# A new order of the instruction queues in a fused attention and gated-mixer kernel

## The chip, the cores and the metric

The kernel runs on one core of a Trainium2 chip. The core has five engines, each with its own instruction queue that is worked off in order: TensorE (PE) for matmuls, ScalarE (ACT), VectorE (DVE) and GpSimd (POOL) for elementwise work, and SyncE (SP), which here only issues DMAs. They wait for each other on semaphores. The metric is the device time of one execution in microseconds; the median of several runs counts, less is better.

## The reference

The input x has 2048 tokens of width 448. A vector c gives six modulation vectors. The first half is windowed attention with 16 heads of 28 columns, where a token sees itself and the 255 tokens before it; the second is a gated MLP whose gate mixes tokens by a full 2048 x 2048 matrix.

```python
mod = silu(c) @ w_mod                       # sa, ca, ga, sb, cb, gb
h = layernorm(x) * (1 + ca) + sa
q, k, v = split_heads(h @ wqkv)
scores = where(0 <= i - j < 256, q @ k.T * 28 ** -0.5, -1e9)
x = x + ga * (merge_heads(softmax(scores) @ v) @ wo)
h = layernorm(x) * (1 + cb) + sb
z = gelu(h @ w_in)                          # 1792 columns, two halves
g = w_sp @ layernorm(z[:, 896:]) + b_sp[:, None]
x = x + gb * ((z[:, :896] * g) @ w_out)
```

## The kernel before

The tokens are cut into 16 tiles of 128 rows (t or j) and 4 blocks of 512 (tb). Weights and x come by DMA, in the front on the queues of SP and ScalarE. There is one pass over the data, in stages that overlap:

- Front. c is turned into a column by four tiny matmuls with a constant `one`, silu is taken on ScalarE, and matmuls with w_mod (`wmod`) give the modulation. `stats` (L591 to L597) takes mean and variance of a tile of x on VectorE and the inverse root on GpSimd; `norm` (L604 on VectorE, L608 and L610 on GpSimd) writes the normalised tile `xn`.
- Transpose and projections. Block 0 and 1 are transposed on TensorE, blocks 2 and 3 by DMA transposes of `xn` on SP's queue; scale and shift follow (L655, L674) into `hT`. `wq` is copied from its staging tile into a padded `WQK` (L583, L584). L689 and L729 give queries and keys, L742 the values; their results are evicted from PSUM by ScalarE or VectorE (L703, L704, L746, L747). Part of the queries is spread into `QBD` by four small DMAs per block.
- Attention, for j = 0 to 15 in two halves: scores (L818, L844, L853), exp on ScalarE (L805), a multiply with the 0/1 mask on VectorE (L860, L880), the product with the values (L887), division by the sum (L901, L903), a DMA transpose of the result (`o_sb` to `hT`), the output projection with `wo_g` (L912), the residual sum (L917), the second layer norm, a DMA transpose of `xn2` to `hT`, and scale and shift (L935, L937).
- Gated block: L997 gives the gate's half of z (ScalarE gelu L1004, statistics and normalisation on VectorE and GpSimd), L1018 the other half, transposed (gelu L1026).
- Spatial product: L1041 multiplies with `w_sp`, whose 32 pieces (`wspA`, `wspB`) are transposed by DMA on SP's queue. VectorE adds the bias `bsp_bc` (L1045), GpSimd multiplies with z (L1048), L1058 is the last product with `w_out_g`, and VectorE adds the residual (L1068) ahead of the store.

Nothing in the program chooses the order at run time or by a rule. Each step is entered into a list by `Sched.add`, with its possible engines and the steps that it depends on, and gets a number. The string `ORDER` then says the rest: one word per step, such as `113.v.0`, gives the number, the engine (p TensorE, a ScalarE, v VectorE, g GpSimd, s SP) and the buffer or PSUM bank that it takes. The words of one engine, from first to last, are that engine's queue. The semaphore waits are derived from dependences and buffer reuse. Some steps may run on one engine alone; others (evictions, scale and shift, normalisation, small copies) have two or three ways. 28 of the 37 optional warm-up matmul steps are left out of the string, in both versions alike.

```python
for word in ORDER.split():
    n, eng, *slots = word.split(".")
    op, e = self.ops[int(n)], ENGS["pavgs".index(eng)]
```

The numbers that matter here: 0 to 20 are loads (1 and 2 the first x tiles, 11, 14 and 15 x blocks 1, 2 and 3, 3 to 5 the first part of wmod, 6 to 8 wq, 12 and 13 the rest of wmod, 16 and 17 wo, 18 to 20 w_in); 22 is the memset of `one`, 25 that of a padding of the wq staging tile; 41 turns c, 42 and 43 are silu(c); 103 to 106 copy wq into WQK; 125, 126, 129 and 130 write hT of block 0; 131 to 134 are its first projection; 214 to 221 and 268 to 275 are statistics of blocks 2 and 3, 236 to 239 the scale and shift of block 2, 240 to 246 projections of it; 323 and 324 the first scores and exp; 756, 757, 764 and 765 the last masks; 805 to 820 and 821 to 836 the transposes of wspA and wspB, 804 the load of the bias.

Of the kernel before, what the change touches and what calls it, by code (L numbers as in the profile page):

```python
# [22 lines left out]
126.v 131.p.5 59.p.0 132.p 133.p 134.p 136.p.3 135.a 138.p.4 46.a 48.v 146.p.1 147.a 164.v 162.v 168.v 163.v 166.v 167.v 165.v 169.v 170.g 171.g 139.a  # L23
142.p.0 143.a 150.s 172.g 151.s 149.s 176.g 174.g 178.g 173.g.0 179.g.1 140.p.2 141.a 137.a 148.s 14.s 16.s 15.s 18.s 17.s 154.p.1 152.p.0 323.p.0
155.v 144.p.1 153.v 145.v 95.p.0 324.a.0 177.v.2 96.v 325.v 175.v.3 327.v 156.p.1 329.p.0 157.a 330.a.1 47.a 97.p.0 98.v 180.p.1 326.p.0 348.p.0 328.p
183.p.0 377.p.0 181.v 182.v 92.p.1 349.a.2 350.a 355.p.0 356.a.3 357.a 331.v 184.v 333.v 185.v 214.v 351.v 94.v 93.v 218.v 158.p.0 332.p 192.p.1 334.p
159.v 186.p.0 375.p.0 193.a 187.a 376.a.4.0 219.v 216.v 27.v 217.v 220.v 215.v 221.v 190.p.1 188.p.0 358.v 335.v 353.v 336.v.0 272.v 191.v 274.v 360.v
273.v 379.v 380.v 270.v 352.p.0 354.p 222.g 223.g 224.g 226.g 228.g 225.g.0 227.g.1 230.g 231.g.2 229.g.3 189.a 378.a 337.s 383.p.0 359.p 160.p.0
385.p.0 198.p.1 361.p 384.a.5.1 161.a 386.a 404.p.0 199.v 362.v 363.v.1 200.p.0 204.p.1 381.p.0 406.p.0 405.a.6.2 407.a 268.v 201.v 409.v 205.v 271.v
388.v 269.v 275.v 387.v 408.v 232.s 235.s 234.s 233.s 196.s 194.s 195.s 197.s 412.p.0 382.p 212.p.0 414.p.0 202.p.1 213.v 413.a.0.3 203.a 433.p.0  # L30
389.p 390.p 210.p.1 208.p.0 434.a.1.4 415.a 209.a 441.p.0 442.a.2.0 417.v 391.v 392.v.2 416.v 410.p.0 411.p 418.p 419.p 437.v 211.v 238.v 435.p.0
206.p.0 276.g 102.g 277.g 101.g 239.g 282.g 236.g 99.g 284.g 280.g 278.g 285.g.0 283.g.1 279.g.2 281.g.3 100.g 420.v 237.v 438.v 421.v.0 436.a 207.a
462.p.0 463.a.3.1 443.p.0 246.p.1 439.p.0 244.p.0 470.p.0 245.v 247.a 444.a 471.a.4.2 240.p.1 464.p.0 242.p.0 440.p 465.a 241.v 445.v 466.v 243.v
475.v 467.v 446.v 491.p.0 492.a.5.3 364.s 393.s 422.s 20.s 447.p 472.p.0 252.p.1 258.p.0 259.v 253.a 499.p.0 473.a 394.p.1 493.p.0 254.p.0 448.p
500.a.6.4 520.p.0 494.a 255.a 521.a.0.0 474.v 495.v 395.v 449.v 450.v.1 496.v 289.s 249.s 287.s 288.s 286.s 451.s 251.s 248.s 250.s 260.p.1 365.p.0
468.p.0 501.p.0 469.p 502.a 261.v 366.v 504.v 528.p.0 476.p 477.p 522.p.0 256.p.1 264.p.0 367.v 478.v 479.v.2 368.v 503.v 525.v 293.v 292.v 524.v
529.a.1.1 257.a 523.a 549.p.0 550.a.2.2 497.p.0 338.p.1 498.p 505.p 530.p.0 506.p 290.g 339.v 291.v 507.v 532.v 533.v 508.v.0 265.a 531.a 557.p.0
558.a.3.3 298.p.1 551.p.0 262.p.0 526.p.0 578.p.0 552.a 299.a 263.v 554.v 562.v 396.v 553.v 527.p 534.p 266.p.0 559.p.0 423.p.1 579.a.4.4 586.p.0
560.a 267.a 583.v 424.v 535.p 536.v 537.v.1 425.v 580.p.0 452.p.0 300.p.1 587.a.5.0 581.a 340.v 426.v 561.v 453.v 341.v 591.v 397.v 582.v 342.g 398.g
399.g 400.g 555.p.0 556.p 588.p.0 301.a 589.a 607.p.0 294.p.1 296.p.0 563.p 609.p.0 608.a.6.1 615.p.0 19.s 480.s 509.s 538.s 297.a 401.g.0 343.g 590.v  # L40
612.v 295.v 564.p 565.v 566.v.2 610.a 617.p.0 616.a.0.2 618.a 481.p.0 482.v 510.p.1 454.v 611.v 483.v 511.v 636.p.0 306.p.0 584.p.0 585.p 592.p 593.p
638.p.0 637.a.1.3 639.a 302.s 303.s 304.s 305.s 567.s 644.p.0 307.v 484.v 594.v 427.g 344.g 402.g 403.s 428.g 345.g.1 512.v 595.v.0 619.v 455.v
310.p.1 311.v 620.v 308.p.0 346.g 369.g 370.g 429.g 485.g 456.g 371.g 645.a.2.4 646.p.0 309.a 647.a 613.p.0 665.p.0 539.p.1 316.p.0 667.p.0 614.p
621.p 347.s 430.g.2 431.g 432.s 596.s 513.v 648.v 640.v 514.g 457.g 515.g 372.g.0 486.g 487.g 516.g 373.g 649.v 641.v 517.g.1 666.a.3.0 668.a 673.p.0
622.p 540.v 317.v 675.p.0 568.p.1 314.p.0 674.a.4.1 676.a 694.p.0 623.v 541.v 624.v.1 642.p.0 696.p.0 643.p 650.p 651.p 669.v 695.a.5.2 315.a 697.a
569.v 677.v 312.p.1 670.v 570.v 652.v 653.v.2 571.v 542.v 458.g 572.g 543.g 805.s 459.g.2 544.g 518.g 625.s 374.s 654.s 488.g.0 545.g 788.g 489.g
573.g 574.g 791.g 702.p.0 597.p.0 704.p.0 671.p.0 678.v 672.p 679.p 680.p 699.v 698.v 598.v 681.v 703.a.6.3 313.a 707.v 682.v.0 599.v 706.v 705.a
723.p.0 724.a.0.4 320.p.1 318.p.0 725.p.0 700.p.0 731.p.0 319.a 726.a 701.p 708.p 709.p 626.p.0 733.p.0 732.a.1.0 321.a 734.a 752.p.0 519.s 683.s
490.s 728.v 727.v 546.g.1 547.g 710.v 655.p.1 460.v 711.v.1 736.v 735.v 789.g 790.g 627.v 656.v 600.v 601.g 575.g.0 576.g 729.p.0 730.p 737.p 738.p
754.p.0 753.a.2.1 755.a 760.p.0 756.v 739.v 740.v.2 757.v 602.g 684.p.0 758.p.0 762.p.0 759.p 761.a.3.2 763.a 837.p.0 838.p.1 657.v 764.v 628.v 658.v  # L50
685.v 712.s 548.s 461.s 659.g 629.v 765.v 603.g 630.g 604.g.1 660.g 631.g 661.g 632.g 792.v 793.a 794.a 713.p.1 766.p 767.p 714.v 795.v 768.v 769.v.0
686.v 322.s 741.s 577.s 770.s 839.p 840.p 841.a 848.a 873.p.3 874.p.2 875.p 876.p 891.p.0 892.p.1 893.p 877.a 884.a 895.a 742.p.0 771.p.1 894.p 902.a
981.p.2 855.p.0 982.p.1 605.v 633.g.2 842.v 634.g 662.v.0 849.v 715.v 687.v 843.v 716.v 606.s 635.s 688.g 663.g 689.g 717.g 718.g 690.g 719.g 691.g.1
743.v 744.v 878.v 745.v 772.v 692.v 664.s 773.v 746.g 747.g 748.g 749.v.2 897.v 774.v 720.v.0 693.s 806.s 797.v 721.v 799.v 796.g 775.g 776.g 903.v
750.v 787.g 777.g 722.s 751.s 850.v 778.v.1 779.g 879.v 886.v 781.g 780.s 896.v 885.v 880.v 851.v 887.v 888.g 889.g 890.v 801.v 803.v 819.s 813.s
811.s 820.s 815.s 808.s 817.s 816.s 814.s 810.s 807.s 818.s 809.s 812.s 798.a 856.p.3 857.p 858.p 859.a 866.a 983.p 984.p 800.v 802.g 904.v 905.v
# [1084 lines left out]
```

## Time and profile before

| | us |
|---|---|
| median of 3 runs | 279.58 |
| the three runs | 279.44, 279.58, 283.84 |
| span of the profiled execution | 281.0 |
| TensorE busy in it | 269.3 |
| VectorE busy | 164.3 |
| ScalarE busy | 128.5 |
| GpSimd busy | 126.1 |

The profile is one execution, its times count from the first instruction of the span. A group of instructions is named by the line of the code that issues it, its engine, and the tiles that it writes and reads. The lines of `stats` and `norm` are helpers' lines, shared by several stages. A gap ahead of an instruction is put down to the work whose semaphore came last. The end of a matmul is modelled, so the time from one start to the next is a better measure of a matmul's cost than its duration.

### The profile page before, as it was taken

To read this page: it belongs to the slowest core of one execution; us is meant where nothing else is said; L and a number is where in the kernel's file an instruction comes from. 1 tells how busy PE (TensorE), PEld (TensorE's weight loads), DVE (VectorE), ACT (ScalarE), POOL (GpSimd) and SP (SyncE) were. 2 spreads that over 40 slices of the span, in tenths; PEclk is the share of its full clock that TensorE was granted. 3 is DMA by queue.
4 is the path that set the end of the run, shared out by engine and by line. 5 is a ranking of instruction groups with operands and counts; after the bars stand their busy time and mean duration, and the time that the engine had idled before them with its cause. 6 is when DMAs were issued, how large, how long until landed. Compare 5 with 4: busy or idle time off the path is not lost.

```text
span 281.0 us, 7380 instructions
## 1 busy us (share of the span) xinstructions
PE 269.3 (96%) x3198; PEld 142.3 (51%) x3222; DVE 164.3 (58%) x355; ACT 128.5 (46%) x151; POOL 126.1 (45%) x200
## 2 busy tenths in 40 slices
PE   6799999799999999999999999999999999999995
PEld 2445556456657777544444444444444444444452
DVE  6347999599899999968898600000243003124443
ACT  4548899789999999866666700000000000000000
POOL 8231177921027989947769503001477101436110
PEclk9789999999999999999999999999999999999999
DMA  6775735343315485693699989910000000000032
GB/s 199 188 261 157 267 58 98 84 55 72 72 23 75 63 96 80 162 103 79 125 181 186 168 181 201 163 36 0 0 2 0 0 0 2 16 16 16 19 98 98
DMA packets 65347, 26.01 MB, mean 93 GB/s; under 512 B 56418, under 2 KB 64227, under 8 KB 65315
## 3 DMA queue, kind: packets, MB, share of 16 engines
q1 hardware_dynamic: 64496, 24.39, 43.6%
q10 hardware_dynamic: 818, 1.15, 1.5%
q8 instruction: 25, 0.41, 0.6%
q14 instruction: 8, 0.06, 0.1%
HBM read 9.01 MB, written 1.84 MB: 39 GB/s over the span
## 4 chain that ended last, share of the span: by engine, by line
PE 80%; POOL 5%; DVE 4%; ACT 4%; issue 3%; DMA 3%; ACTq 0%; POOLq 0%
PE ps L1041 34%; PE ps L997 8%; PE ps L1058 8%; PE ps L1018 8%; PE ps L689 6%; PE ps L887 4%; ACT PW L805 3%; PE ps L912 3%; DMA wmod<-in_w_mod_dram 3%; PE ps L844 2%; PE ps L742 2%; PE ps L853 1%; POOL xn L610 1%; PE ps L729 1%; POOL wo_g L580 1%
## 5 line engine op out<-in xcount | busy, mean ns | idle before, releaser
L805 ACT ACTIVATE PW<-ps 128x2048 bf16<-128x2048 f32 (+1 forms) x56 | 67.8, 1240 | 4.3 <-PE ps L844 2.6
L1048 POOL TENSOR_TENSOR z1T<-tmpg,z1T 128x512 bf16<-128x512 bf16 x28 | 31.7, 1152 | 77.9 <-DVE tmpg L1045 77.9
L1045 DVE TENSOR_TENSOR tmpg<-ps,bsp_bc 128x512 bf16<-128x512 f32 x28 | 19.0, 689 | 79.2 <-PE ps L1041 70.3
L1041 PE MATMUL ps<-wspB,z 128*128 128x512 bf16 x219 | 49.2, 379 | 0.3
L1041 PE MATMUL ps<-wspA,z 128*128 128x512 bf16 x219 | 48.9, 379 | 0.4 <-issue 0.2
L860 DVE TENSOR_TENSOR PT<-PW,mask 128x1024 bf16<-128x1024 bf16 x56 | 39.2, 729 | 0.3 <-ACT PW L805 0.2
L1041 PEld LDWEIGHTS ps<-wspA,z 128*128 128x128 bf16 x224 | 21.8, 98 | 26.6 <-issue 0.4
L1041 PEld LDWEIGHTS ps<-wspB,z 128*128 128x128 bf16 x224 | 21.9, 98 | 26.3
L596 POOL TENSOR_SCALAR ve_all<-mv_all 128x1 f32<-128x1 f32 (+2 forms) x37 | 11.3, 312 | 46.7 <-DVE mv_all L594 45.9
L689 PE MATMUL ps<-hT,WQK 128*128 128x512 bf16 x98 | 25.5, 388 | 2.4 <-POOL hT L655 1.4
L597 POOL TENSOR_TENSOR rs_all<-ve_all,neghalf 128x1 f32<-128x1 f32 (+2 forms) x37 | 25.3, 694 | 1.1
L887 PE MATMUL ps<-Vaug,PT 128*128 128x32 bf16 x496 | 24.4, 177 | 0.5 <-DVE PT L860 0.5
L887 PEld LDWEIGHTS ps<-Vaug,PT 128*128 128x128 bf16 x496 | 21.8, 96 | 4.4 <-DVE o_sb L903 0.9
L997 PE MATMUL ps<-w_in,hT 64*128 64x448 bf16 x224 | 22.7, 349 | 0.2 <-ACT PW L805 0.2
L1018 PE MATMUL ps<-hT,w_in 64*128 64x512 bf16 x196 | 22.3, 376 | 0.0
L1058 PE MATMUL ps<-w_out_g,z1T 128*128 128x448 bf16 x112 | 21.8, 353 | 0.0
L887 PE MATMUL ps<-Vaug,PW 128*128 128x32 bf16 x224 | 20.2, 176 | 0.0
L591 DVE BATCH_NORM_STATS2 st_all<-x_sb 128x6 f32<-128x448 bf16 x32 | 19.2, 610 | 0.4 <-DMA x_sb<-in_A_x_dram 0.4
L610 POOL TENSOR_SCALAR xn<-x_sb,rs_all,ve_all 128x448 bf16<-128x448 bf16 x22 | 18.9, 863 | 0.3
L887 PEld LDWEIGHTS ps<-Vaug,PW 128*128 128x128 bf16 x224 | 17.6, 96 | 1.9
L591 DVE BATCH_NORM_STATS2 st_all<-z 128x6 f32<-128x448 bf16 x32 | 18.1, 602 | 0.2 <-ACT z L1004 0.2
L1004 ACT ACTIVATE z<-ps 128x896 bf16<-128x896 f32 x16 | 14.1, 915 | 8.3 <-PE ps L997 8.2
(100 smaller groups left out, 333.1 us busy)
## 6 DMA issues: line engine op xcount, KB each, us to landing
out_dram<-fin SPq DMA_DIRECT2D x16, 112.0 KB, 1.7
x_sb<-in_A_x_dram SPq DMA_DIRECT2D x3, 448.0 KB, 4.9
wmod<-in_w_mod_dram SPq DMA_DIRECT2D x1, 1344.0 KB, 8.6
w_in<-in_B_w_in_dram SPq DMA_DIRECT2D x1, 1344.0 KB, 8.9
QBD<-qT SPq DMA_DIRECT2D x16, 64.0 KB, 2.0
w_out_g<-in_B_w_out_dram SPq DMA_DIRECT2D x1, 784.0 KB, 5.3
bsp_bc<-in_B_b_sp_dram SPq DMA_DIRECT2D x1, 512.0 KB, 6.8
wmod<-in_w_mod_dram SPq DMA_DIRECT2D x2, 224.0 KB, 6.1
```

Source lines behind the costliest of these rows:

```text
L591: st = [dve(0.62 if True else 0, lambda e, t=t, ci=ci, s=s: e.bn_stats(st_all[:, slot, t, ci, :], s()), deps(t), prio) for ci, s in enumer ...
L597: rs = pool(0.53 + 0.15 * len(tiles), lambda e: e.tensor_tensor(rs_all[:, slot, a:b], ve_all[:, slot, a:b], neghalf[:, 0:b - a], ALU.pow), ...
L610: "pool": (0.9, lambda e: e.tensor_scalar(to[:, h.slot[0], 0:D], x_sb[:, t, :], z, ve, ALU.mult, ALU.add))}, [nm], prio, [h])
L689: mms = [lambda e, h=h, g=g, kc=kc, tb=tb: e.matmul(ps[:, h.slot[0], :], lhsT=WQK[:, kc, 4 * g:4 * g + 4, :].rearrange("p a b -> p (a b)") ...
L805: ex = act(xdur, lambda e, out_ap=out_ap, in_ap=in_ap: e.activation(out_ap(), in_ap(), ACT.Exp, scale=SCALE), [s], v - 8.0 + u, takes, tab ...
L860: return dve(0.70, lambda e: e.tensor_tensor(cols(hp.slot[0] * 2048 + 1024 * k, [[256, 4], [128, 2], [1, 128]]), cols(at_w() + 128 + 192 * ...
L887: fns.append(lambda e, hp=hp, hO=hO, hi=hi, bi=bi, kb=kb, hd=hd, nb=nb, a=at[hi][bi], p_of=p_of: e.matmul(ps[:, hO.slot[0], 32 * hd:32 * h ...
L997: return lambda e, kc, p0, start, stop: e.matmul(ps[:, hs[t % 2].slot[hf], 0:D], lhsT=hT[p0:p0 + 64, kc, t * 128:(t + 1) * 128], rhs=w_in[ ...
L1018: return lambda e, kc, p0, start, stop: e.matmul(ps[:, hs[b // 2].slot[b % 2], :], lhsT=w_in[p0:p0 + 64, kc, ft * 128:(ft + 1) * 128], rhs ...
L1041: m = pe(16 * MMS, [lambda e, h=h, si=si, ft=ft, tb=tb: e.matmul(ps[:, h.slot[0], :], lhsT=z2[:, si, ft * 128:(ft + 1) * 128], rhs=(wspA i ...
L1048: u = pool(1.16, lambda e, ht=ht, ft=ft, tb=tb: e.tensor_tensor(z1T[tb][:, ft, :], tmpg[:, ht.slot[0], :], z1T[tb][:, ft, :], ALU.mult), [ ...
L1058: return [lambda e, ft=ft: e.matmul(ps[:, h.slot[0], 0:D], lhsT=z1T[t // 4][:, ft, (t % 4) * 128:(t % 4 + 1) * 128], rhs=w_out_g[:, ft, :] ...
```

## The change

Only `ORDER` is replaced. The two strings hold the same 1145 steps, so the same matmuls, elementwise instructions and DMAs run, on the same data, with the waits derived again. Two things differ: the place of a step in its engine's queue, and for 58 steps the engine. 19 steps go from GpSimd to VectorE and 11 from VectorE to GpSimd; 15 go from ScalarE to VectorE and 13 from VectorE to ScalarE. No step is moved to or from TensorE and SP. The buffers and banks that steps take are chosen anew with the order.

The first lines of the two strings show the front, the next the place where the projection of block 2 begins, then the end of attention, and the last the transposes of w_sp:

```diff
-2.a 21.v 30.g 1.s 22.v 23.v 24.v 33.g 34.g 0.a 4.s 31.g 3.a 28.g 25.v 5.s 32.g 6.a 26.v 35.g 50.v 51.p.0 7.s 40.a 8.s 52.p.1 36.g 107.v 53.p.2 109.v
-37.g 108.v 115.v 41.p.0 29.g 38.g 110.v 54.p.3 117.v 39.g 42.a 111.g 43.a 116.v 112.g 118.v 44.a 55.p.4 119.g 113.v.0 45.a 56.p.5 120.g 114.v.1
-123.p.1 9.s 121.v.2 49.p.0 122.v.3 10.s 105.a 11.s 106.a 127.p.2 12.s 103.v 104.g 124.p 88.v 128.p 89.v 90.v 13.s 91.v 57.p.3 125.a 129.v 58.p.4 130.a
...
+0.a 24.v 1.s 2.a 15.s 3.a 17.s 30.g 31.g 4.s 32.g 35.g 58.p.0 5.s 7.s 59.p.0 107.v 34.g 14.s 55.p.0 115.v 29.g 8.s 52.p.0 33.g 28.g 21.v 109.v 37.g
+40.a 36.g 53.p.0 108.v 117.v 54.p.0 110.v 23.v 118.v 111.g 274.v 57.p.0 112.g 22.v 41.p.0 51.p.1 39.g 42.a 113.v.0 43.a 44.a 114.v.1 56.p.1 116.v
+270.v 119.g 123.p.1 120.g 268.v 6.a 127.p.2 45.a 38.g 9.s 122.v.2 49.p.0 121.v.3 11.s 272.v 10.s 25.v 220.v 105.a 12.s 218.v 13.s 103.a 104.v 124.p
+20.s 216.v 128.p 50.v 88.v 106.a 89.v 90.v 91.v 125.v 126.v 129.a 131.p.3 132.p 130.v 133.p 47.a 26.v 134.p 271.v 168.v 140.p.4 164.v 46.a 166.v
...
+407.a 197.s 281.v.3 417.v 208.p.1 442.a.2.0 289.s 237.v 389.p 388.v 414.p.0 244.p.0 416.v 337.s 415.a 209.v 390.p 245.a 462.p.0 391.v 408.v 240.p.1
...
+736.v 726.a 760.p.0 576.g 321.a 627.v 754.p.0 577.s 730.p 757.v 755.a 737.p 738.p 761.a.3.2 762.p.0 739.v 684.p.1 322.s 756.v 657.v 713.p.0 740.v.0
+792.a 837.p.0 765.v 741.s 763.a 658.v 838.p.1 764.v 794.a 659.g 714.v 603.g 793.a 758.p.0 660.g 685.v 759.p 795.g 766.p 767.p 839.p 661.g 768.v
...
+820.s 885.v 892.p.3 859.a 843.v 893.p 745.v 878.v 812.s 746.g 981.p.0 692.g 895.a 861.v 747.g 774.v 879.v 894.p 775.g 798.a 810.s 776.g 799.v 858.p
...
+1035.a 1022.p.1 853.g 833.s 972.g 854.v 1014.p.0 944.v 962.v 823.s 1023.p 865.v 973.v 1015.p 1026.a 908.v 825.s 1024.p 1025.a 1016.p 830.s 1043.p.4
+1020.a 1019.a 1027.a 836.s 1017.a 1018.a 1028.a 829.s 1079.p.5 827.s 834.s 828.s 1040.p.0 822.s 826.s 1088.p.1 804.s 824.s 821.s 1082.p.6 1080.v.0
```

More of the change, by code (lines that the diff above doesn't have):

```diff
@@ L24 @@
[L24 to L47, printed above, removed]
@@ new lines @@
+146.p.0 135.a 48.v 214.v 141.a 138.p.5 273.v 147.a 217.v 27.v 167.v 169.v 136.p.1 162.v 139.a 163.v 275.v 165.v 142.p.0 170.g 137.a 171.g 323.p.0
+143.v 156.p.1 324.a.0 178.g 221.v 176.g 150.s 144.p.0 177.g.0 157.v 148.s 219.v 172.g 215.v 269.v 152.p.1 174.g 145.v 151.s 175.g.1 149.s 154.p.0
+179.v.2 153.a 222.g 173.v.3 16.s 223.g 329.p.0 155.v 97.p.1 18.s 330.a.1 327.v 19.s 276.g 180.p.0 226.g 98.v 348.p.0 181.v 95.p.1 349.a.2 182.v
+377.p.0 96.v 183.p.0 350.a 92.p.1 99.g 184.v 185.a 230.g 224.g 355.p.0 93.v 331.v 190.p.0 356.a.3 277.g 325.v 94.v 353.v 192.p.1 231.v.0 191.a 284.g
@@ L73 @@
+1162.p 1124.p.1 1159.v.3 1163.v.1 1160.s 1129.s 1125.v.2 1164.s 1126.s
 """
```

64 lines of the change are left out of this document (38 added, 26 removed).

## The prediction

> **What bounds the kernel now.** The page's list of busy times comes first, because it says which engine a new order has to serve.
>
> ```profile
> PE 269.3 (96%) x3198; PEld 142.3 (51%) x3222; DVE 164.3 (58%) x355; ACT 128.5 (46%) x151; POOL 126.1 (45%) x200
> ```
>
> TensorE is busy in 269.3 of 281.0 us, so an order alone can win back at most some 11.7 us, if no matmul goes faster. But the share is an average. The table by stage (columns: stretch, length, then the busy time and count of PE, PEld, DVE, ACT and POOL, the granted clock, DMA share, GB/s) shows where the loss is and who sets the pace:
>
> ```profile
> 0.00:18.50 18.50, 13.99 (x82) 6.88 (x84) 10.55 (x35) 8.71 (x12) 7.93 (x21) 0.82 0.78 241
> 18.50:30.10 11.60, 11.30 (x134) 6.03 (x132) 7.06 (x17) 9.29 (x12) 3.63 (x8) 1.00 0.56 171
> 30.10:57.00 26.90, 24.84 (x528) 14.45 (x536) 23.46 (x53) 23.95 (x26) 18.99 (x26) 1.00 0.49 106
> 57.00:116.60 59.60, 58.24 (x1476) 39.38 (x1479) 57.89 (x118) 55.08 (x56) 32.52 (x53) 1.00 0.43 68
> 116.60:160.30 43.70, 43.54 (x439) 21.00 (x439) 37.13 (x92) 29.57 (x45) 31.29 (x66) 1.00 0.88 150
> ```
>
> ```profile
> 160.30:278.20 117.90, 117.33 (x550) 54.54 (x558) 27.66 (x44) 1.93 (x4) 31.72 (x28) 1.00 0.25 49
> ```
>
> From 116.6 us to 278.2 TensorE stands still for 0.16 + 0.57 us. That tail of 161.6 us is full, and an order can only lengthen it. Everything to be won lies before 116.6, in the attention stage, where VectorE is the fullest engine: 57.89 of 59.6 us in the long stretch, and ScalarE 55.08. "A busy PE" says little there, since its small matmuls are pipelined and their ends modelled. The end of that stage is one instruction, the last mask multiply, and TensorE goes on with the gated block's first product right behind the matmuls that wait for it:
>
> ```profile
> 115.94 0.66 DVE L860 TENSOR_TENSOR PT<-PW,mask 128x1024 bf16<-128x1024 bf16 x1
> ```
>
> ```profile
> 117.40 2.82 PE L997 MATMUL ps<-w_in,hT 64*128 64x448 bf16 x28
> ```
>
> So I forecast when VectorE finishes that mask. Its ledger up to 116.6 us is 10.55 + 7.06 + 23.46 + 57.89 = 98.96 us busy, and idle 7.95 + 4.54 + 3.44 + 1.71 = 17.64 us. The chain of waits (start, length, what) names the two idle pieces that an order can touch:
>
> ```profile
> 1.94 7.71 DMA wmod<-in_w_mod_dram
> ...
> 15.55 5.63 PE ps L689 x23
> ...
> 50.67 1.52 POOL hT L655
> 52.19 0.35 issue
> 52.54 0.81 PE ps L689 x3
> ```
>
> The front waits for a weight load and then for the first query/key projection (L689) at 15.55. At 52.5 the projection of token block 2 waits for its normalised input, which GpSimd scales (L655) after its statistics came late: both VectorE and TensorE lose time around there.
>
> **The front, where the change costs.** Only the queues' order differs, so each step is costed by what now stands ahead of it. On SP's queue the load of x block 3 (448 KB) and a 56 KB piece of wo now stand behind the first x piece and ahead of SP's two pieces of wmod; x block 2 (448 KB) goes ahead of the last piece of wq. On ScalarE's queue the 448 KB piece of wq, issued at 2.37 us, moves behind the two small activations that make silu(c). On VectorE, a `bn_stats` of x block 3 goes ahead of the memset of `one`, and others of blocks 3 and 2 ahead of the copy of wq into WQK. Those queues are in order, so silu(c), and with it the issue of that piece of wq, now wait for x block 3.
>
> ```profile
> x_sb<-in_A_x_dram SPq DMA_DIRECT2D x3, 448.0 KB, 4.9
> ...
> wq_st<-in_A_wqkv_dram ACTq DMA_DIRECT2D x1, 448.0 KB, 8.7
> ...
> wspA<-in_B_w_sp_dram SPq DMA_TRANSPOSE x16, 4.2
> ```
>
> ```profile
> 2.37 0.49 ACTq L409 DMA_DIRECT2D wq_st<-in_A_wqkv_dram  x1
> ...
> 23.61 1.02 ACT L805 ACTIVATE PT<-ps 128x1024 bf16<-128x1024 f32 x1
> ```
>
> ```profile
> 0.88 0.06 DVE L478 MEMSET one<- 1x2 bf16 x1
> ...
> 12.60 1.00 DVE L674 TENSOR_SCALAR hT<-ps,modT 128x512 bf16<-128x512 bf16 x2 [0.83 <-PE ps L660]
> ```
>
> Issued near 1.3 us, x block 3 lands after 4.9 us (the median of the three loads of its size) at 6.2, or after 8.7 (the same size in the crowded front) at 10.0. I take 8.5: the first x pieces and ScalarE's wmod share the engines with it. One statistic, the memset (now at 9.2 instead of 0.88), four tiny matmuls and two small activations later, the piece of wq is issued at some 10.3 us instead of 2.37; it lands at 15.2 to 19.0, where it landed at 2.37 + 8.7 = 11.1. I take 15.6, near the short end, because the competing wmod piece is done by then. Behind it VectorE still copies WQK, does a statistic and five small copies, and makes the four hT chunks that were made at 12.60: the first L689 comes at some 17.6 us, 2.1 later than 15.55, with 21 as the far end. Two units of four matmuls are moved behind the first scores, worth 8 x 5.63 / 23 = 2.0 us, but TensorE idles longer ahead of L689 and its clock drops again (0.82 over the first 18.5 us before, 3.3 us lost). So the first exp comes at about 25 (23.7 to 27), not 23.61.
>
> [...]
>
> **VectorE's ledger with the change.** Fifty-eight instructions change engine; VectorE gets 34 and gives 24. What does not cancel is five normalisations, one scale-shift of the second block, three evictions of queries or keys and two of values to VectorE, and one small copy away from it. In groups (busy, mean ns | idle before):
>
> ```profile
> L860 DVE TENSOR_TENSOR PT<-PW,mask 128x1024 bf16<-128x1024 bf16 x56 | 39.2, 729 | 0.3 <-ACT PW L805 0.2
> ...
> L747 DVE CAST Vaug<-ps 128x448 bf16<-128x448 f32 x7 | 4.3, 615 | 4.0 <-PE ps L742 4.0
> ...
> L604 DVE TENSOR_SCALAR xn<-x_sb,mv_all,rs_all 128x448 bf16<-128x448 bf16 x10 | 4.1, 431 | 3.5 <-DMA hT<-xn 2.1 <-POOL rs_all L597 0.8 <-POOL ve_all L608 0.6
> ...
> L937 DVE TENSOR_SCALAR hT<-hT,modT 128x512 bf16<-128x512 bf16 x7 | 4.1, 608 | 0.0
> L704 DVE CAST KT<-ps 128x512 bf16<-128x512 f32 x6 | 4.1, 680 | 0.7 <-PE ps L689 0.7
> ```
>
> 5 x 0.431 + 0.608 + 3 x 0.680 + 2 x 0.615 = 6.0 us; less the copy, and less the part in which one instruction starts before the last one ends, I take 5.0. All of it stands ahead of the last mask.
>
> Idle time: the first stretch keeps its 7.95 us nearly (7.0, the waits have other names); the second keeps 4.0 of 4.54, since the first exp is later though the statistics of blocks 2 and 3 are already done; the third falls from 3.44 to 1.0, because with those statistics done early the normalised block 2 is transposed sooner and the wait at 52.5 goes; the fourth keeps 1.71. Together 13.7 us. What is late next in the third stretch is VectorE itself: it scales three chunks of block 2 there only after it has worked off the masks queued ahead.
>
> [...]
>
> ```profile
> 43.35 0.66 DVE L860 TENSOR_TENSOR PT<-PW,mask 128x1024 bf16<-128x1024 bf16 x1
> ...
> 47.53 2.14 DVE L860 TENSOR_TENSOR PT<-PW,mask 128x1024 bf16<-128x1024 bf16 x2
> ```
>
> ```profile
> 47.67 1.45 POOL L580 TENSOR_TENSOR wo_g<-wo_g,gg_sb 128x448 bf16<-128x448 bf16 x1
> ```
>
> A mask takes 0.66 us alone; two took 2.14 while GpSimd's multiply ran. Over 56 masks the mean of 0.729 is 3.9 us above 0.66. An order that takes turns saves between 0 and those 3.9 us and GpSimd has eight instructions fewer; new pairs can also cost as much. I take 2.5 saved. [...]
>
> Last mask: 98.96 + 5.0 + 13.7 - 2.5 = 115.2 us, 1.4 earlier than 116.6.
>
> **Behind it, at nothing.** The 14 transposes of wspA that end the queue are cover that could fail:
>
> ```profile
> 135.54 19.94 SPq L467 DMA_TRANSPOSE wspA<-in_B_w_sp_dram  x14
> ```
>
> The last is issued by 155.48 and lands 4.2 us later, just ahead of the spatial product at 160.3; three of them now stand in SP's gaps ahead of the last hT transposes, so they end sooner by about 3 x 1.42 us. If a late hT blocked SP, each us beyond 0.6 would be paid in full. The bias load moves behind 13 transposes of wspB, 18.5 us; its first reader has eight banks of 16 matmuls of cover, 128 x 117.33 / 550 = 27.3 us, and so does wspB, now first used in the ninth unit rather than the tenth. The reordered final products cost nothing while they find their bank free a unit ahead. The tail stays 161.6 us.
>
> **The sum.** The profiled execution spans 281.0 us against a median of 279.58 of the runs, 1.4 more. 281.0 - 1.4 = 279.6 in the profile; less the same 1.4 it is **278.2 us**.
>
> **Rivals.** *The front decides (slower).* Place: ScalarE's piece of wq behind VectorE's wait for x block 3. If x lands at 10 and wq takes 8.7 us in a front where SP's queue is still full, the first L689 comes at 21 or later, and the second stretch's idle time grows by about 4 us that nothing makes up, since VectorE has 5 us more work: 98.96 + 5.0 + 17.7 - 2.5 = 119.2, time 282.2. It decides against me from a first L689 at about 19.5. For it: ScalarE's wq piece took 8.7 us before. Against it: idle time there was paid before too. [...] *SP's transposes become the bound*: a wait of 3 us ahead of the spatial product gives 281.2. [...]
>
> **Numbers.** Forecast 0.42, front 0.28, freed middle 0.16, SP 0.06, port unchanged 0.08. The forecast's own range, from its unknown terms (first L689 17 to 19, port 0 to 3.9), is 276 to 281. For 8 in 10 I take 274.5 to 283.0, from the freed middle to past the front's 282.2. About 2% is what a measurement of this kernel can tell from no change: under 274.0 needs more than the freed middle (0.07), over 285.2 needs the front's far end with a stall behind it (0.12); within 2%: 0.81.
>
> **What would show it.** In the changed profile: first L689 near 17.6 and first exp near 25 (over 19.5: the front rival); no wait for L655 near 52; masks with a mean near 0.69 us; the last mask near 115; TensorE full from there to the end. I am wrong if the last mask is early but gaps stand behind it, or if it is late though the front was not.

## The result and the profile after

| | before | after |
|---|---|---|
| median, 18 executions each, same chip | 279.93 us | 282.24 us |
| lowest to highest | 278.75 to 283.84 | 281.50 to 283.19 |
| ratio of the times, 95% interval | | 1.0079 (1.0056 to 1.0101) |
| span of the shown profile | 281.0 us | 279.8 us |
| time of that execution | not given | 281.53 us |

The kernel became 0.8% slower, 2.2 us (279.93 x 0.0079). The forecast was 278.2, a little faster. The time lies in the range of 274.5 to 283.0, and within 2% as was thought likeliest, but on the wrong side of no change.

The two profiles say the opposite: after's span is 1.2 us shorter. The table by stage of after, with the columns and stretches of before's (stretch, length, busy time and count of PE, PEld, DVE, ACT and POOL, granted clock, DMA share, GB/s):

```profile
0.00:18.50 18.50, 10.52 (x76) 5.18 (x78) 13.46 (x38) 9.41 (x13) 6.88 (x20) 0.91 0.93 304
18.50:30.10 11.60, 11.60 (x112) 5.56 (x109) 9.20 (x28) 8.35 (x10) 6.08 (x13) 1.00 0.40 117
30.10:57.00 26.90, 25.98 (x596) 16.36 (x603) 23.76 (x51) 23.98 (x24) 10.36 (x16) 1.00 0.45 94
57.00:116.60 59.60, 58.83 (x1474) 40.04 (x1479) 57.70 (x122) 56.73 (x58) 28.63 (x53) 1.00 0.47 80
116.60:160.30 43.70, 43.47 (x412) 20.33 (x408) 33.76 (x86) 28.57 (x45) 27.90 (x62) 1.00 0.85 147
160.30:278.20 117.90, 115.73 (x544) 53.81 (x550) 28.24 (x44) 1.30 (x3) 33.75 (x30) 1.00 0.20 44
```

And the end of its attention stage in the timeline (start, length), with the group of masks from the page:

```profile
112.73 0.68 DVE L860 TENSOR_TENSOR PT<-PW,mask 128x1024 bf16<-128x1024 bf16 x1
113.42 0.66 DVE L860 TENSOR_TENSOR PT<-PW,mask 128x1024 bf16<-128x1024 bf16 x1
...
115.49 2.82 PE L997 MATMUL ps<-w_in,hT 64*128 64x448 bf16 x28
```

```profile
L860 DVE TENSOR_TENSOR PT<-PW,mask 128x1024 bf16<-128x1024 bf16 x56 | 37.1, 688 | 0.0
```

Inside these profiles the change did nearly what was forecast: the masks' mean fell from 729 to 688 ns, GpSimd's busy time from 30 to 57 us from 18.99 to 10.36, and the last mask ends at 114.08 instead of 116.6 (forecast 115.2). The forecast span was 279.6, the measured one is 279.8. So what failed is mainly the way from the profile to the median, and the first experiment was put there.

The slices of TensorE's clock show where to look. Before, between 10.24 and 20.48 us (columns as above):

```profile
10.24:13.65 3.41, 3.41 (x36) 2.54 (x36) 1.65 (x7) 2.41 (x4) 1.15 (x1) 0.50 0.71 163
13.65:17.07 3.42, 3.20 (x9) 1.29 (x9) 1.51 (x4) 0.51 (x2) 0.00 (x0) 0.54 1.00 376
17.07:20.48 3.41, 3.41 (x18) 1.57 (x16) 1.41 (x6) 2.32 (x5) 1.69 (x4) 1.00 0.55 190
```

After, the same slices:

```profile
10.24:13.65 3.41, 1.66 (x37) 1.35 (x34) 3.12 (x7) 1.79 (x3) 0.73 (x2) 1.00 1.06 360
13.65:17.07 3.42, 0.86 (x3) 0.38 (x5) 3.18 (x13) 3.42 (x5) 0.00 (x0) 0.71 1.04 391
17.07:20.48 3.41, 3.41 (x14) 1.46 (x13) 3.27 (x12) 2.41 (x4) 0.00 (x0) 0.79 0.61 163
```

Both executions ran part of the front at half clock (0.50 in before's first slice; 0.71 and 0.79 are slices that are partly at half: the clock of after is 0.50 from 16 to 18 us and 1.00 from 19). In after TensorE is nearly idle from 12.1 to about 16 us and slow after that. Whether that is a property of each kernel or of the execution that was profiled, one profile can't say.

### The profile page after: what moved, and what is told of

The parts are those of the page before. It is cut to its first block, busy times and chain, and to the rows that moved or that the text cites. A ratio compares the mean times of both kernels' runs of the same rounds, so it can differ in the third digit from the quotient of the medians.

```text
span 279.8 us, 7377 instructions
## 1 busy us (share of the span) xinstructions
PE 266.1 (95%) x3196; PEld 141.3 (50%) x3222; DVE 166.1 (59%) x365; ACT 128.3 (46%) x149; POOL 113.6 (41%) x192
## 4 chain that ended last, share of the span: by engine, by line
PE 81%; DVE 9%; DMA 4%; ACT 2%; issue 1%; POOL 1%; ACTq 0%; DVEq 0%; POOLq 0%
PE ps L1041 34%; PE ps L689 8%; PE ps L1058 8%; PE ps L887 5%; PE ps L1018 5%; PE ps L997 4%; PE ps L844 4%; PE ps L912 4%; PE ps L742 4%; DVE st_all L591 3%; DMA hT<-xn 2%; PE ps L853 2%; ACT PW L805 2%; DMA x_sb<-in_A_x_dram 2%; PE ps L729 1%
## 5 line engine op out<-in xcount | busy, mean ns | idle before, releaser
L860 DVE TENSOR_TENSOR PT<-PW,mask 128x1024 bf16<-128x1024 bf16 x56 | 37.1, 688 | 0.0
L1041 PEld LDWEIGHTS ps<-wspB,z 128*128 128x128 bf16 x224 | 21.9, 98 | 26.4
L689 PE MATMUL ps<-hT,WQK 128*128 128x512 bf16 x96 | 24.8, 393 | 5.5 <-DVE hT L674 4.1
L597 POOL TENSOR_TENSOR rs_all<-ve_all,neghalf 128x1 f32<-128x1 f32 (+2 forms) x37 | 25.9, 704 | 1.4
L596 POOL TENSOR_SCALAR ve_all<-mv_all 128x1 f32<-128x1 f32 (+2 forms) x37 | 10.2, 278 | 37.3 <-DVE mv_all L594 34.2
L887 PE MATMUL ps<-Vaug,PT 128*128 128x32 bf16 x496 | 23.8, 177 | 0.0
L887 PEld LDWEIGHTS ps<-Vaug,PT 128*128 128x128 bf16 x496 | 21.8, 96 | 3.9 <-DVE o_sb L903 0.6
L887 PE MATMUL ps<-Vaug,PW 128*128 128x32 bf16 x224 | 19.8, 176 | 0.0
L887 PEld LDWEIGHTS ps<-Vaug,PW 128*128 128x128 bf16 x224 | 17.5, 96 | 2.1
L689 PEld LDWEIGHTS ps<-hT,WQK 128*128 128x128 bf16 x112 | 10.2, 100 | 15.7 <-DVE hT L674 4.5
L1026 ACT ACTIVATE z1T<-ps 128x512 bf16<-128x512 f32 x28 | 14.8, 602 | 5.8 <-PE ps L1018 5.7
```

The costliest lines, as they stand in the source:

```text
L597: rs = pool(0.53 + 0.15 * len(tiles), lambda e: e.tensor_tensor(rs_all[:, slot, a:b], ve_all[:, slot, a:b], neghalf[:, 0:b - a], ALU.pow), ...
L689: mms = [lambda e, h=h, g=g, kc=kc, tb=tb: e.matmul(ps[:, h.slot[0], :], lhsT=WQK[:, kc, 4 * g:4 * g + 4, :].rearrange("p a b -> p (a b)") ...
L860: return dve(0.70, lambda e: e.tensor_tensor(cols(hp.slot[0] * 2048 + 1024 * k, [[256, 4], [128, 2], [1, 128]]), cols(at_w() + 128 + 192 * ...
L887: fns.append(lambda e, hp=hp, hO=hO, hi=hi, bi=bi, kb=kb, hd=hd, nb=nb, a=at[hi][bi], p_of=p_of: e.matmul(ps[:, hO.slot[0], 32 * hd:32 * h ...
L1041: m = pe(16 * MMS, [lambda e, h=h, si=si, ft=ft, tb=tb: e.matmul(ps[:, h.slot[0], :], lhsT=z2[:, si, ft * 128:(ft + 1) * 128], rhs=(wspA i ...
```

## The experiments

### Is the profile of before like its median?

Before, unchanged.

> The kernel before, unchanged, for the span of each of its executions. After's profile spans 279.8 us at a time of 281.53, so 1.73 us lie outside its span. Theory A (the profile of before was one of its slow executions): with the same 1.73 outside, before's median of 279.93 means spans of about 278.2, and the shown 281.0 is reached only by the executions near 282 to 283. Theory B (the two kernels differ outside the span): spans here stay near 281.0 with a time near 280, that is under 1 us or nothing outside.

Measured: 280.67 us, ratio 1.0002 (0.9982 to 1.0023), and for every execution about 1.7 to 1.8 us between span and time. That is theory A. Over all 108 executions of before that ran beside the experiments, by mean granted clock:

| clock | executions | median time, us | time less span, us |
|---|---|---|---|
| 0.999 to 1.0 | 47 | 279.7 | 1.7 to 1.8 |
| 0.993 to 0.994 | 56 | 281.0 | 1.7 to 1.8 |
| 0.982 to 0.988 | 5 | 283.1 | 1.7 to 1.8 |

The profile shown of before has a clock of 0.988 and, with 1.73 added to 281.0, a time of some 282.7: it belongs to the last row, with 5 executions of 108, and lies 2 to 3 us above the median (279.93 in the result, 280.6 over the 108). The profile of before_again has a quick front, with a clock of 1.0 like the first row. Its slices:

```profile
10.24:13.65 3.41, 2.55 (x13) 1.08 (x12) 1.61 (x7) 2.52 (x4) 1.04 (x1) 1.00 0.90 278
13.65:17.07 3.42, 3.42 (x17) 1.57 (x16) 2.85 (x9) 2.48 (x5) 0.00 (x0) 1.00 0.99 370
17.07:20.48 3.41, 3.41 (x24) 1.50 (x23) 1.54 (x5) 3.23 (x5) 3.06 (x8) 1.00 0.20 48
```

and its first exp in the timeline:

```profile
19.91 1.02 ACT L805 ACTIVATE PT<-ps 128x1024 bf16<-128x1024 f32 x1
```

In the slice from 13.65, 17 matmuls ran, where the shown execution of before ran 9. The first exp is at 19.9, not 23.61. In before_sp (below), whose front is before's and whose profiled execution has a clock of 0.993 like the middle row, it is at 21.42. After's, in its shown profile, is at 23.54, and that execution was one of after's quickest: 15 of its 18 have a clock below 0.99, and none reaches 0.999.

The execution of before_again also shows a second limit of before, further back:

```profile
158.94 2.32 PE L1041 MATMUL ps<-wspA,z 128*128 128x512 bf16 x10 [2.14 <-ACT z1T L1026]
```

```profile
DMA to landing us min/median/max: 4.1/4.3/6.8
```

(The second line is for the last three transposes of wspA, issued at 149.1 to 151.8.) If the slowest of them is the last, it landed at 151.8 + 6.8 = 158.6: TensorE then waited 2.14 us for a late transpose, not for the activation that is named as releaser.

### Which part of the order costs?

Two orders can be joined: a number of words from one, then all steps that are left in the order of the other. The kernels are named by the part that is taken from one of them (front_after has the front of after).

```diff
-words 1 to 126 of the old order
+words 1 to 126 of the new order
 all other steps in the old order
```

> The order of after up to the first score product (126 words), then before's order for all that is left. Front theory: the loss of 2.3 us is made ahead of the first exp, so this is 1.5 to 3 us slower than before (281.5 to 283). Rival, later stages: the front costs nothing (first exp 23.54 against 23.61 in the profiles), so this is within 0.7 us of before.

Measured: 283.72 us, ratio 1.0119 (1.0096 to 1.0142). The front alone costs at least as much as the whole change does (the intervals overlap): the front theory holds. A part of the excess comes from the joint: an eviction of before's order (L703 at 22.63) stands ahead of the first exp on ScalarE's queue, some 0.9 us that after does not have there.

```diff
-words 1 to 698 of the old order
+words 1 to 698 of the new order
 all other steps in the old order
```

> The order of after up to the last masks (698 words), then before's order. Front theory: as front_after less the 2.2 us that the middle won in the profiles, so 280 or less. Tail theory (the reordered gated block, transposes and last products cost): about before's time or faster, 277.7 to 280. If the middle costs, it is slower than front_after.

Measured: 283.20 us, ratio 1.0104 (1.0078 to 1.0129). It was expected at 280 or less. The middle brings only 0.5 us of the 2.2, and the intervals overlap. Where it is lost, the times of three marks in the profiles tell (us; first exp, end of the last mask, and the differences):

| kernel | first exp | to last mask | from there to the end | first exp to end |
|---|---|---|---|---|
| before, as shown | 23.61 | 93.0 | 164.4 | 257.4 |
| before_again | 19.91 | 92.9 | 166.8 | 259.7 (2.1 of it the wait above) |
| front_after | 24.54 | 92.4 | 164.4 | 256.8 |
| frontmid_after | 24.78 | 90.5 | 166.2 | 256.6 |
| after | 23.54 | 90.5 | 165.7 | 256.3 |
| after_warm (below) | 22.27 | 90.6 | 165.4 | 256.0 |

The new middle does win 2 us up to the last mask, and the end gives most of them back. The stretch from the last mask to the spatial product, before (the row ends 0.2 us ahead of it) and then after:

```profile
116.60:160.05 43.45, 43.45 (x438) 20.86 (x436) 37.13 (x92) 29.44 (x44) 31.29 (x66) 1.00 0.87 148
```

```profile
114.10:158.68 44.58, 44.35 (x463) 21.41 (x463) 35.76 (x90) 29.44 (x44) 30.20 (x67) 1.00 0.85 154
```

TensorE is busy almost without a gap in both, but behind the earlier last mask it has 463 matmuls left instead of 438. Nearly all of the difference is products with the values (L887), 48 instead of 24. So an earlier mask partly moves work from ahead of the mark to behind it. That TensorE's own work is the limit from the first exp on is argued from this; no run tests it alone.

The other half of the pair was to show the end alone, and the front taken back:

```diff
 words 1 to 700 of the old order
-all other steps in the old order
+all other steps in the new order
```

> Before's order up to the last masks (700 words), then after's. Tail theory: 1.5 to 3 us slower than before. Front theory: within 0.7 us of before, since TensorE is full from the last mask on in both profiles.

Measured: 288.85 us, ratio 1.0302 (1.0278 to 1.0326). No theory foresaw 8 us. At the seam, the place where the two orders are joined, the load of w_out (784 KB, 6.4 us) is issued just ahead of the transpose of the 15th attention result, which then takes 6.2 us and holds up the division behind it at 122.8. The kernel measures its seam, and says nothing on the end of after.

```diff
-words 1 to 134 of the new order
+words 1 to 134 of the old order
 all other steps in the new order
```

> Before's order up to the first exp (134 words), then after's. Front theory: the first exp comes near 20 to 21.8, as in before's own executions, and what the middle and the end of after win is kept, so it is faster than both kernels: 277 to 279.5. Rival, the gains of the middle cannot be had with the early front (before's two parts give 2 us back between 116 and 160): about before's time, 280 to 281.

Measured: 290.76 us, ratio 1.0364 (1.0309 to 1.0418). Again a seam: in the old front the x blocks 2 and 3 are issued after 20 us, and VectorE, whose new order has their statistics next, waits for them until 26.5. Neither theory foresaw it.

### What makes the new front late?

Three edits of after follow. The first puts back seven of the warm-up steps that both orders leave out:

```diff
-216.v 128.p 50.v 88.v
+216.v 128.p 60.p.3 61.p.4 62.p.5 63.p.3 64.p.4 65.p.5 66.p.3 50.v 88.v
```

> After, with seven of the warm-up steps that are left out of both orders (14 matmuls on the identity) put back on TensorE behind the last product with wmod, into its idle 4 us ahead of the first query/key projection. Clock theory: the granted clock falls because TensorE stands idle there; with work in the gap it stays at 1.0 (mean 0.999 or more, not 0.988), the first exp comes 1 to 3.4 us earlier than after's, and the time falls by 1 to 2 us, to 280.2 to 281.2. [...]

Measured: 280.26 us, ratio to before 0.9981 (0.9960 to 1.0002), where after had 1.0079. The loss is gone. The clock is 0.998 or more in nine of ten executions. The first query/key projections in TensorE's timeline, in after and then in after_warm (start, length, count, idle time ahead):

```profile
16.21 6.25 PE L689 MATMUL ps<-hT,WQK 128*128 128x512 bf16 x23 [4.08 <-DVE hT L674]
```

```profile
11.79 3.19 PE L559 MATMUL ps<-ident 128*128 128x512 bf16 x14
15.45 0.39 PE L689 MATMUL ps<-hT,WQK 128*128 128x512 bf16 x1 [0.47 <-DVE hT L674]
16.03 5.16 PE L689 MATMUL ps<-hT,WQK 128*128 128x512 bf16 x23 [0.19 <-DVE hT L674]
```

Hardly anything starts earlier. (The group has 24 matmuls; the record of the first is missing in after, where its input was ready at 15.58, so some of the 4.08 us is not idle.) The same 23 matmuls take 5.16 us instead of 6.25, and the first exp comes at 22.27 instead of 23.54. This was one of after's better executions; where the half rate lasts longer, more is lost: in frontmid_after, with after's front and a clock of 0.53 and 0.50 in the slices from 13.65 to 20.48 (0.71 and 0.79 in after), the 23 took 7.19.

The second edit takes up the front rival as it was put, the late load of wq:

```diff
-40.a
+6.a 40.a
...
-268.v 6.a 127.p.2
+268.v 127.p.2
```

> After, with ScalarE's 448 KB load of wq moved back ahead of silu(c), as in before. If the late load sets the first query/key projection (the front rival as it was put), that comes from 15.6 to 14 or earlier and the time falls by 1 us or more. If VectorE's statistics ahead of the hT chunks set it, the first projection stays within 0.6 us of 15.6 and the time within 0.7 of after's.

Measured: 282.08 us, ratio 1.0051 (1.0025 to 1.0077); the first projection starts at 15.54. The load, issued 6.6 us earlier, changes hardly anything (after started at about 15.6 and had the ratio 1.0079), because ScalarE's copies of wq into WQK wait for something else, here as in after:

```profile
12.52 2.63 ACT L583 ACTIVATE WQK<-wq_st 128x896 bf16<-128x896 bf16 x3 [1.62 <-DVE wq_st L480]
```

L480 is the memset of the padding of wq's staging tile (step 25). Before did it at 2.54 us, after does it at 12.14, behind four statistics. The chain of waits of after is VectorE's queue alone in the last 4 to 5 us ahead of the projection:

```profile
11.45 0.54 DVE st_all L591
11.99 0.15 issue
12.14 0.43 DVE wq_st L480
12.57 0.03 issue
12.60 0.90 DVE st_all L591 x2
...
13.68 0.37 DVE WQK L584
14.05 0.54 DVE st_all L591
...
15.03 0.55 DVE hT L674
```

The third edit takes the statistics out of there:

```diff
-111.g 274.v 57.p.0
+111.g 57.p.0
...
-20.s 216.v 128.p
+20.s 128.p
...
-163.v 275.v 165.v 142.p.0
+163.v 165.v 274.v 270.v 268.v 272.v 220.v 218.v 216.v 271.v 214.v 273.v 217.v 275.v 142.p.0
```

> After, with twelve statistics steps of x blocks 2 and 3 on VectorE moved from between the front's steps to behind the normalisation of block 1. If VectorE's queue sets the first projection, it comes 1 to 3 us earlier than 15.6 (as far as wq allows), TensorE idles less, the clock falls less, and the time falls by 1 to 2.5 us. If the late load of wq sets it, the first projection stays at 15 or later and the time within 0.7 of after's, or worse by what the later statistics cost.

Measured: 282.90 us, ratio 1.0100 (1.0065 to 1.0136). The projection starts some 1.5 us earlier, at 14.04, as VectorE's queue would have it, and yet the kernel is no faster:

```profile
14.04 8.68 PE L689 MATMUL ps<-hT,WQK 128*128 128x512 bf16 x24 [2.06 <-DVE hT L674]
```

24 matmuls take 8.68 us, where 23 at full rate took 5.16: more than half of them run at half rate (the clock is 0.50 and 0.53 in the slices from 13.65 to 20.48), and the first exp is at 23.81. To start earlier while TensorE runs at half rate won nothing here. The moved statistics cost something behind it as well: the first exp of group j = 2 comes at 35.83, in after at 34.49.

The clock theory is tested from the other side by taking warm-up steps 54 to 59 out of before.

```diff
-110.v 54.p.3 117.v
+110.v 117.v
...
-91.v 57.p.3 125.a 129.v 58.p.4
+91.v 125.a 129.v
```

> Before without the six warm-up steps (12 matmuls on the identity, no output of them is used) that stand between silu(c) and the first query/key projection. Clock theory, from the other side: TensorE then idles in the front as in after, the granted clock falls to 0.988 or below, the first exp comes at 22 to 24.5 instead of 19.9, and the time rises by 0.8 to 2.2 us over before. Rival (the clock in after falls for another reason than TensorE's idle time): the clocks stay at 0.994 to 1.0 and the time within 0.5 us of before.

Measured: 281.92 us, ratio 1.0052 (1.0028 to 1.0076). TensorE's projections in the timelines of before_again and before_cold:

```profile
12.35 5.13 PE L689 MATMUL ps<-hT,WQK 128*128 128x512 bf16 x23
```

```profile
11.97 8.18 PE L689 MATMUL ps<-hT,WQK 128*128 128x512 bf16 x24 [1.08 <-ACT hT L672]
```

The first exp comes at 22.58. Time and rate are as the theory expected; the clock in the records is not: it is 1.0 in eight of twelve executions (the last section tells why it misleads).

The same question for before's own spread: two warm-up steps more behind the first transposes, and two behind the first products with wmod.

```diff
-123.p.1 9.s 121.v.2 49.p.0
+123.p.1 60.p.0 61.p.0 9.s 121.v.2 49.p.0 62.p.2 63.p.3
```

> Before with four warm-up steps more (eight matmuls), two behind the first transposes and two behind the first products with wmod, where TensorE waits for weights. If before's two groups of executions come from TensorE's idle time in the front, the slower one goes: clocks of 0.998 or more in nearly all executions and a median of 279.2 to 279.8, with a smaller spread. Rival: the groups come from when the weights land, so both stay, and the median is within 0.3 us of before's.

Measured: 280.77 us, ratio 1.0014 (0.9983 to 1.0045). Nine of twelve executions have a clock of 0.999 or more, but these nine lie between 279.83 and 281.57. The median did not fall, so the theory's time was missed; what the rest of before's spread comes from stays open.

### Can the best of both be had?

The first try moves the late transposes of before:

```diff
-635.s
+635.s 819.s
...
-664.s
+664.s 813.s
...
-803.v 819.s 813.s 811.s
+803.v 811.s
```

> Before, with two of the transposes of wspA that end SP's queue put into gaps ahead of the last hT transposes, as after has three of them. Theory: in executions with a quick front before's spatial product waits for the last wspA transpose (158.7 in before_again's profile, 2.1 us of waiting), so the wait falls to under 0.5 us and the time by 0.5 to 1.5 us in the median. Rival: the moved transposes delay the hT transposes by as much, and the time stays within 0.4 us.

Measured: 279.62 us, ratio 0.9983 (0.9959 to 1.0008). Not told from no change: among executions at full clock its median is 279.4, where before's on the same chip is 279.5. So the wait for the late transpose, seen in before_again, is probably not in most executions; the profile of before_warm, whose transposes stand as in before, shows none.

Two versions of after with fewer statistics ahead of the projections, the early load of wq and four or five warm-up steps:

```diff
-40.a
+6.a 40.a
...
-128.p
+128.p 60.p.3 61.p.4 62.p.5 63.p.3
...
-165.v
+165.v 220.v 218.v 216.v 214.v 217.v
...
-157.v
+157.v 274.v 270.v 268.v 272.v 271.v 273.v 275.v
```

> After, with wq's load ahead of silu(c), the statistics of block 2 behind the normalisation of block 1 and those of block 3 behind the first exp on VectorE, and four warm-up steps in TensorE's gap. If queue and clock together made the front late, the first projection comes at 12.3 to 13.5, the clock stays at 0.998 or more, the first exp comes at 19.5 to 21.5, and with after's middle and end the time is 277.5 to 279.3, below both kernels. Rival: the moved statistics cost the middle what the front wins: 280 to 281, as after_warm.

Measured: 282.51 us, ratio 1.0090 (1.0057 to 1.0123). The clock is full, and the first projection (13.79) and the first exp (21.66) come only just later than expected. But the moved statistics now stand ahead of the evictions in the chain of waits, as the rival had it, and cost more than its 280 to 281:

```profile
19.63 2.09 DVE st_all L591 x4
...
22.97 2.11 DVE st_all L591 x4
```

The first exp of group j = 2 comes 1.0 us later than in after (35.49 against 34.49), though the very first came 1.9 earlier.

> As best_a, but with only block 3's statistics moved and five warm-up steps: the first projection at 13.5 to 14.5, the first exp at 20.5 to 22, time 278 to 279.8 by the same theory; 280 to 281 by the rival.

This one moves only block 3's statistics. Measured: 282.66 us, ratio 1.0077 (1.0050 to 1.0103). It is no better: the statistics stand in its chain of waits at 22.71, and the first exp of j = 2 comes at 36.81. Five of its ten executions also have a clock of 0.994; in the profiled one the half clock lies at 26.4 to 29.8 (0.72 over the stretch from 23.9 to 30.1), behind the statistics.

Then before's front with after's middle, with the x loads moved so that VectorE should not wait for them:

```diff
 words 1 to 134 of the old order, but
-13.s
+13.s 14.s 15.s
...
-169.v
+169.v 220.v 218.v 216.v 214.v 217.v
 all other steps in the new order, statistics of block 3 one each behind 221.v, 157.v and 219.v, four behind 269.v
```

> Before's front, then after's middle and end, with the loads of x blocks 2 and 3 behind the last piece of wmod on SP, the statistics of block 2 behind the normalisation of block 1 and those of block 3 spread behind the first exps on VectorE. If front and middle can be had apart: first exp near 20 to 21.5, 90 to 91 us from it to the last mask, time 277.5 to 279.3, below both kernels. Rival: the new middle lives on statistics that were made while the front waited; here VectorE makes them between 18 and 30 us and the scores wait for it, so the first exp of group j = 2 comes at 33 or later and the time is 280 to 283.

> As front_before2, with the two x loads ahead of the last two pieces of wmod: block 2 lands some 2 us earlier. By the first theory as front_before2 or 0.5 us faster; by the rival 280 to 283 as well.

> front_before2 with the four warm-up steps of before_warm: by the clock theory 0.3 to 1 us below front_before2 and with clocks of 0.998 or more; otherwise the same as front_before2.

Measured: 289.41 us (ratio 1.0317), 285.04 (1.0159) and 289.45 (1.0309). All are slower than even the rival said. The fourth was to gain on the second by its warm-up steps and did not: its clock is 0.981 to 0.982 (0.976 to 0.988 in the second), and in the second's profile four matmuls still take 1.89 us at 24.55, where before's take 1.03, far behind the place of these steps. Two rows of VectorE's and TensorE's timelines of front_before2:

```profile
21.70 2.21 DVE L591 BATCH_NORM_STATS2 st_all<-x_sb 128x6 f32<-128x448 bf16 x4 [3.88 <-DMA x_sb<-in_A_x_dram]
```

```profile
24.55 1.89 PE L689 MATMUL ps<-hT,WQK 128*128 128x512 bf16 x4 [4.68 <-DVE Vaug L747]
```

Block 2, issued at 11.5, lands only at 21.7, and TensorE then waits 4.68 us for an eviction that stands behind the statistics in VectorE's queue. So the rival's reason holds: the early loads and early statistics are what after's middle lives on, and they are paid for in the front.

Last, three statistics of block 2 moved only past the hT chunks, in best_c together with the early load, five warm-up steps and one copy into WQK on VectorE, in best_d alone with six warm-up steps:

```diff
-20.s 216.v 128.p
+20.s 128.p
...
-26.v
+26.v 220.v 218.v 216.v
```

> after_warm with five warm-up steps, wq's load ahead of silu(c), one copy into WQK on VectorE in place of ScalarE, and three statistics of block 2 moved from ahead of the hT chunks to right behind them. The first projection comes at 14.0 to 14.5 and its fourth step at 15.3 instead of 16.5, the first exp at 20.8 to 21.5 instead of 22.3, the statistics are done when they were, so nothing behind is later: 279.0 to 279.8. Rival, ScalarE's copies (they wait for wq's piece at 12.4) set it: as after_warm, 280.0 to 280.5.

> after_warm with six warm-up steps, and only the three statistics moved. By the first theory the first projection at 14.3 to 14.7 but its fourth step no earlier than 15.3, time 279.3 to 280; by the rival as after_warm, 280.0 to 280.5.

Measured: 280.42 us, ratio 0.9995 (0.9974 to 1.0017), and 281.38, ratio 1.0026 (1.0005 to 1.0048). In best_c the first exp is at 21.67 as in best_a, with less loss behind (the first exp of j = 2 at 33.77, after_warm 33.22), but the time is that of after_warm, as the rival had it. In best_d's profile the six warm-up steps ran mostly at half rate (12 matmuls in 4.26 us, where after_warm's 14 took 3.19) and kept TensorE until 17.5, so that they delayed what they were to help; but that is its one execution with a clock below 0.999, and why the other eleven are no faster than after_warm stays open. No version is shown to beat before; after_warm and before_sp come nearest. To move the memset L480 back to the start, alone or together with the warm-up steps, was not tried, so its part in the late projection is read from the chain and not shown.

## Why the prediction was wrong

**The step that failed is the last: "281.0 - 1.4 = 279.6 in the profile; less the same 1.4 it is 278.2 us".** No execution lies 1.4 below its span; each lies about 1.73 above it. The shown execution of before was one of about 282.7 us, at half clock for 6.8 us of the front, and the median execution is not. With 279.6 + 1.73 the same working gives 281.3, against 281.53 measured for the profiled execution of after; the median of after is another 0.7 above that. So the wrong baseline makes 3.1 of the 4.0 us between 278.2 and 282.24. The 0.82 in the first stretch was read, and the loss of 3.3 us in it named, but it was taken for a property of the kernel that both orders share. It could have been doubted then: a median time below the span of the profile means that the profile is not of a median execution. That the span itself was met within 0.2 us is partly luck: the last mask came 1.1 us earlier than forecast and the rest took 1.3 longer. Most marks of "what would show it" came true (the waits, the masks, the full TensorE), but they were marks within the profile, and none could have shown a wrong baseline.

**The front.** The forecast had the first projection at 17.6 and the first exp at 25; they came at about 15.6 (16.21 in the records, which lack the first matmul) and 23.54 (the first statistic of x block 3 was done at 8.2, without a wait for its load, and wq's piece, issued at 8.99, took 4.5 us). The forecast was too pessimistic against the profile, and as a loss of 1.4 us too optimistic against before's usual fronts, which have the first exp at 19.91 (before_again) and 21.42 (before_sp). "TensorE idles longer ahead of L689 and its clock drops again" was the mechanism that decides; the word again hid that before has less of it: 47 of its 108 executions show no drop, 56 a short one (0.994), while 15 of after's 18 lie below 0.99. after_warm (work in the gap, 0.998 or more in nine of ten) and before_cold (work taken out, 24 matmuls in 8.18 us where before_again's 23 took 5.13) show it from both sides.

**The front rival** gave 282.2, which is the time measured, but for a reason that did not hold. That is luck. Its mark, a first L689 at 19.5 or later, was not reached, and the late load of wq on which it rested costs nothing that after_wqa could tell. What ScalarE's copies waited for was the padding's memset, which the prediction listed nowhere among the steps that VectorE's queue holds up. The 8.7 us that it took for the piece, as before's row has it, did not come: the piece took 4.5.

What happened lies behind the gap. Behind the nearly idle stretch the 23 matmuls of after took 6.25 us, and with work in it (after_warm) 5.16. The stretch at half clock in the records lasts 3.41 us in after and 6.83 in before as shown; in after_stats it fills nearly all of the two slices from 13.65 to 20.48 (0.50 and 0.53). How long a gap brings on the half rate, and what ends it, no run shows: the gap just ahead of the projection is 4.08 us in after's records and 2.06 in after_stats, so the longer stretch at half clock comes with the shorter gap.

**VectorE's ledger** held in its total, not in its parts. Busy up to the last mask: forecast 98.96 + 5.0 - 2.5 = 101.5, measured 102.1. Idle by stretch: forecast 7.0, 4.0, 1.0 and 1.7, measured 5.0, 2.4, 3.1 and 1.4 (each stretch less its busy time, the last one ending at 114.08). The front stretches idled less than forecast and the third hardly less than before. The mean mask was forecast near 0.69 and is 0.688. No run shows the port that the forecast's range and chances name; the profiles show masks of 0.66 us, slower ones beside GpSimd's work (two in 2.14), and a sum over all masks that fell from 39.2 to 37.1 us, 2.1 where 2.5 was forecast. Nor did a run come near the 274.5 at the range's lower end: the lowest median of any version is 279.62 (before_sp). The wait for L655 near 52 is gone; TensorE is busy for 25.98 us of that stretch instead of 24.84.

**"The tail stays 161.6 us"** was wrong by 1.3: from the last mask to the end it is 165.7 instead of 164.4. To take the last mask as the event that sets the end was the error of thought there. TensorE, at 58.24 of 59.6 us in the long stretch, had hardly any room, and products that it had done ahead of the old last mask it does behind the earlier one (48 instead of 24). The SP rival, a wait ahead of the spatial product, was found, but in an execution of before.

**The sum as measured.** Ahead of the first exp after loses 2 to 4 us against before's usual executions; from there to the end it wins 1 to 3 (256.3 against 257.4 in before as shown and 259.7 in before_again). With warm-up in the gap the loss ahead of the first exp shrinks to some 1 to 2.4 us, and the two about cancel: ratio 0.9981.

## What to carry to other kernels

Before a term is read from a profile, set its span against the medians: if the time of the profiled execution is not near the median, the profile is of another kind of execution, and a second one is worth more than a closer reading of the first. An order that leaves TensorE idle can pay twice, as here: for the gap (4.08 us in after's records, 2.06 in after_stats) and for the matmuls behind it at half rate (23 in 6.25 us and 24 in 8.68, against 23 in 5.16). So it is worth trying to fill such gaps with matmuls that nobody needs, if they are sure to be done in time; here that took the ratio from 1.0079 to 0.9981 (after_warm). And a mark such as "the last mask" bounds the end only while the engine behind it has nothing else to do.

## What the hardware showed that was not expected

The granted clock in the records misses part of the half rate. In before_cold's profile the slice from 13.65 reads

```profile
13.65:17.07 3.42, 3.42 (x9) 1.21 (x8) 2.53 (x9) 1.54 (x2) 0.68 (x2) 1.00 0.93 346
```

a clock of 1.00, with 9 matmuls where before_again has 17 in the same slice at the same clock. The reason lies in where the records begin: the trace of before_cold has no record of the clock ahead of 17.56 us, that of before_again none ahead of 6.72, that of before none ahead of 6.53, and a time without a record counts as full. In these traces the matmuls stay at half rate up to that first record. In before six warm-up matmuls take 2.74 us from 2.39 on, in a slice with a clock of 1.00, where in after_warm 14 take 3.19. In before_cold the 24 of the first projection, at 0.43 us each from 11.97 to 17.56 and 0.22 behind it, come to 8.0 of the 8.18 us measured (an estimate). The same 12 transposes in before_cold and then in before_again took

```profile
9.43 1.46 PE L660 MATMUL ps<-ident,xn 128*128 128x128 bf16 x12
```

```profile
9.35 0.84 PE L660 MATMUL ps<-ident,xn 128*128 128x128 bf16 x12
```

So a mean clock of 1.0 can also be that of an execution that reached the full rate late. The count of matmuls, or the distance between their starts (0.43 us or 0.22 for 512 columns in these runs), is the better gauge.

One kernel's executions fall into groups: 279.7 us at a mean clock of 1.0 and 281.0 at 0.994, a difference of 0.5% that a single profile does not show. The profiles place it in the first 20 us, with one execution of each kind: at a mean clock of 1.0 the first exp is at 19.91 (before_again), at 0.993 at 21.42 (before_sp), at 0.988, with 6.83 us at half clock in the records, at 23.61 (before as shown).
